# Token blocks of 384 in the second product, and a different order of the float64 pieces in the first step

## The chip, the cores and the metric

The kernel runs on one core of a Trainium2 chip. The metric is the device time of one execution in microseconds (us), the median of several runs. PE is the matrix engine (TensorE) and PEld its weight loads, which run beside its products. DVE (VectorE), ACT (ScalarE) and POOL (GpSimd) are the elementwise engines, SP issues the transfers (DMA). Matrix products are written to banks of PSUM, from which only DVE and ACT read here.

## The reference

```python
def sm_attn(qq, kk, vv):                      # scale = 1/8
    s = scale * np.matmul(qq, kk.transpose(0, 1, 3, 2))
    s = s - np.max(s, axis=-1, keepdims=True)
    a = np.exp(s)
    a = a / (np.sum(a, axis=-1, keepdims=True) + 1e-09)
    return np.matmul(a, vv)
...
p_packed = sm_attn(p, k, v)                   # q, k, v: 8 x 8 x 576 x 64, p: 8 x 8 x 32 x 64
out = sm_attn(q, p_packed, p_packed)
...
x = attn_out.transpose(0, 2, 1, 3).reshape(4608, 512)
x = (x @ w_a) * (x @ w_b) @ w_out             # 512 -> 1536 -> 512
h = x @ w_in                                  # 512 -> 2048
return (h * np.clip(h + 3.0, 0.0, 6.0) / 6.0) @ w_out2   # 2048 -> 512
```

The weights of the three dense products arrive as float64 and are rounded on the chip.

## The kernel before

The kernel has two halves. The first does the attention and the gated product with `w_a`, `w_b` and `w_out`; the second does `w_in`, the gate and the last product, with sums of blocks in place of some products. The change is in the first half.

**The first half.** The 4608 tokens are four groups `g` of two batch entries `b`, 576 tokens each. A step `t` is one group and one of the 12 slices of 128 of the middle width 1536, so there are 48 steps. The attention weights of a batch entry (`at`, on 256 rows, as a high and a low part `at_hi`, `at_lo`) are not multiplied with the packed values first. Instead `pw_unit` forms, for a step, the packed values times the weights `w_a` and `w_b` (`pw`, split into `pw_hi` and `pw_lo`), and `ab_unit` multiplies this with the attention weights. Each product of two split operands is three matrix products, high by high, high by low and low by high (`mm3`, lines 59 to 61).

A step has four `ab` units, two for each batch entry (`b` 0 or 1, half `h` 0 or 1). Before, each unit covers 288 tokens: two banks of six products, ACT copies the first bank to `a` (line 434), DVE multiplies `a` with the second bank to `g32` (line 436), and two ticks later ACT rounds to `g_hi` (line 442) and POOL forms `g_lo` (line 443). A tick is a counter that is advanced after every unit of PE work. There are three banks for `ab`, two for `y` (the second product) and three shared ones (`att`), of which a `pw` takes two.

**The second product.** `y_unit` takes three steps at a time: for one 128-slice `oc` of the 512 outputs and one token block `r` it makes nine products of 128 x 128 weights with the block of `g`. Before, a block is 288 tokens, four blocks for a group. The sum over the four sets of three steps stands in `acc` (lines 460 to 463) and goes to DRAM as `y1d`.

**Float64 pieces.** A piece is 128 x 512 of a weight matrix in float64. Rounding one takes two passes on ACT (lines 81, 82), three on DVE (lines 84, 88, 93) and one on POOL (line 96). Pieces `(m, 0)` and `(m, 1)` are the two halves of the `w_a` and `w_b` slice of step m, `(m, 2)` is its slice of `w_out`. All of them are rounded in the first 12 steps (group 0), a step ahead of use or more; five come even before step 0. `wo_split` then splits a `w_out` slice into a high and a low part.

**Order.** Every engine works through its own list in the order of the program; the loop over steps writes that order by hand. In each step come the units `ab` (0,0), `pw` of the next step, `ab` (0,1), `ab` (1,0), `ab` (1,1). After each there are two slots into which parts of pieces (`parts`), units of the next group's attention (`todo`) and a `y` unit are put. Some units of steps 0 and 1 are done ahead, in a prologue.

Of the kernel before, what the change touches and what calls it, by code (L numbers as in the profile page):

```python
# [8 lines left out]
F32 = mybir.dt.float32  # L9
F32R = mybir.dt.float32r  # L10
# [9 lines left out]
B, H, S, D, NP = 8, 8, 576, 64, 32  # L20
NT = B * S
DM, F1, F2 = 512, 1536, 2048
P = 128
NM1 = F1 // P
NM2 = F2 // P
SH = S // 2
NG = B // 2
TG = 2 * S
SW = 3
# [11 lines left out]
def f32(ap):  # L41
    return ap.bitcast(F32)
# [3 lines left out]
def tile_kernel(ctx: ExitStack, tc: tile.TileContext, qT, kT, vn, pT, wab, wo1, win, wo2, out):  # L46
# [9 lines left out]
    act, dve, pool, pe, sp = nc.scalar, nc.vector, nc.gpsimd, nc.tensor, nc.sync  # L56
# [223 lines left out]
    def at_split(b, cs=(0, 1)):  # L280
        if b not in at_t:
            at_t[b] = (
                main.tile([P, 2, S], F32R, tag="at_hi", name=f"at_hi{b}", bufs=3),
                main.tile([P, 2, S], F32R, tag="at_lo", name=f"at_lo{b}", bufs=3),
            )
        hi, lo = at_t[b]
        for c in cs:
            a = at32_t.pop((b, c))
            act.copy(hi[:, c, :], a)
            pool.tensor_sub(lo[:, c, :], a, f32(hi[:, c, :]))  # L290

    def loads(b):

# [33 lines left out]


    first = [(0, 0), (0, 1), (1, 0), (1, 1), (2, 0)]
    pieces = first + [(2, 1), (0, 2), (1, 2), (3, 0)]  # L330
    for m in range(1, NM1):
        pieces += [x for x in ((m + 2, 1), (m + 1, 2), (m + 3, 0)) if x[0] < NM1]
    n_first = len(pieces)
    pieces += [(NM1 + m, w) for m in range(NM2) for w in range(2)]
    raw64 = {}
# [85 lines left out]
    def ab_unit(t, b, h):  # L421
        hi, lo = pw_t[t]
        ath, atl = at_t[2 * (t // NM1) + b]
        r = 2 * b + h
        ps = []
        for w in range(2):
            pt = psum.tile([P, 512], F32, tag="ab", name=f"ab{t}_{r}{w}", bufs=BANKS["ab"])[:, :SH]
            for c in range(2):
                ws = slice(w * P, (w + 1) * P)
                ts = slice(h * SH, (h + 1) * SH)  # L430
                mm3(pt, hi[:, c, b, ws], lo[:, c, b, ws], ath[:, c, ts], atl[:, c, ts], c == 0, c == 1)
            ps.append(pt)
        a = main.tile([P, SH], F32, tag="a", name=f"a{t}_{r}", bufs=2)
        act.copy(a, ps[0])  # L434
        g32 = main.tile([P, SH], F32, tag="g32", name=f"g32_{t}_{r}", bufs=3)
        dve.tensor_mul(g32, a, ps[1])  # L436
        gh = main.tile([P, SH], F32R, tag=f"g_hi{r}", name=f"g_hi{t}_{r}", bufs=SW + 1)
        gl = main.tile([P, SH], F32R, tag=f"g_lo{r}", name=f"g_lo{t}_{r}", bufs=SW + 1)
        g_t[t, r] = (gh, gl)

        def rest():
            act.copy(gh, g32)  # L442
            pool.tensor_sub(gl, g32, f32(gh))  # L443
            if t % SW == SW - 1:
                later(2, lambda: y_ready.extend((t // NM1, t % NM1 // SW, oc, r) for oc in range(DM // P)))

        later(2, rest)

    y_ready = []

    def y_unit(g, s, oc, r):
        ps = psum.tile([P, 512], F32, tag="y", name=f"y{g}_{s}{oc}{r}", bufs=BANKS["y"])[:, :SH]
        for i in range(SW):
            t = g * NM1 + s * SW + i
            gh, gl = g_t[t, r]
            oh, ol = wo_t[t, oc // 2]
            ws = slice(oc % 2 * P, (oc % 2 + 1) * P)
            mm3(ps, oh[:, ws], ol[:, ws], gh, gl, i == 0, i == SW - 1)
        if s == 0:
            acc_t[oc, r] = main.tile([P, SH], F32, tag=f"acc{oc}{r}", name=f"acc{g}_{oc}{r}", bufs=1)  # L460
            act.copy(acc_t[oc, r], ps)
        else:
            dve.tensor_add(acc_t[oc, r], ps, acc_t[oc, r])  # L463
        if s == NM1 // SW - 1:
            sp.dma_start(y1d[oc, :, g * TG + r * SH:g * TG + (r + 1) * SH], acc_t[oc, r])

# [125 lines left out]
    def spread(work, n):  # L592

        return [work[len(work) * i // n:len(work) * (i + 1) // n] for i in range(n)]
# [69 lines left out]
    def ahead_by_one(starts):  # L664
# [8 lines left out]
            units.append(unit)  # L673
        return units

    for t in range(NSTEP):
        g, m = divmod(t, NM1)
        if m == 0 and g + 1 < NG:
            lhs_tiles(g + 1)
            b = 2 * g + 2  # L680
            u0, u1 = att_units(b), att_units(b + 1)
            bg = u0 + u1[:1] + [lambda b=b: at_split(b, (0,))] + u1[1:2] + [lambda b=b: at_split(b, (1,))] + u1[2:]
        if m == 0 and g + 1 == NG:
            sp.dma_start(*stores[-1])
            es_att.close()
            p2a = es_p2a.enter_context(tc.tile_pool(name="p2a", bufs=1, side="right", reuse_waits="tile"))
            y_load, y_first, y_part = y_units(p2a, 0)
            wo_load0, wo_parts0 = wo_prep(p2a, 0)
# [13 lines left out]

        if t == 0:
            n_conv = 4
        elif g == 0:
            n_conv = sum(x < NM1 for x in (m + 2, m + 1, m + 3))
        else:
            n_conv = 2 * NM2 * (t - NM1 + 1) // (2 * NM1) - 2 * NM2 * (t - NM1) // (2 * NM1) if g < 3 else 0
        parts = spread(list(range(5 * n_conv)), 9 if n_conv > 2 else 6) + [[]] * 4
        now = []  # L710
        for i, (u, *x) in enumerate(units):
            if (u.__name__[:2], *x) not in ahead:
                u(*x)
            tick()
            if i == 1:
                wab_load(t + 3)
            if m % SW < 2 and i in ((3, 4) if t == 0 else (1, 2)):
                wo_split(t, i - (3 if t == 0 else 1))
            if m % SW == 1 and i == 4:
                wo_split(t + 1, 0)  # L720
            if m % SW == 2 and i == 1:
                wo_split(t, 1)
            if i in (3, 4) and m == NM1 - 1 and g + 1 < NG:
                at_split(2 * g + 3, (i - 3,))
            for k in range(2):
                for _ in parts[2 * i + k]:
                    if not now:
                        now = piece_units()
                    now.pop(0)()
                for fn in todo[2 * i + k]:  # L730
                    fn()
                if y_ready and (k == 0 or i in (1, 3)):
                    y_unit(*y_ready.pop(0))
                    tick()
    while due or y_ready:
# [193 lines left out]
```

## Time and profile before

| | |
|---|---|
| median of 3 runs | 1561.6 us (1560.71 to 1562.37) |
| the profiled execution | 1560.16 us, of which the trace's span is 1558.4 us |
| PE busy | 1491.6 us, 96% of the span |
| DVE, ACT, POOL busy | 56%, 44%, 32% of the span |
| mean granted clock of PE | 0.986 of full speed |

A matrix product is pipelined, so the time that PE is called busy overlaps itself: what one product takes out of the engine's time is the distance from its start to the next start, not its duration. An engine's idle time costs something only where another engine, in the end PE, waits for it. Names are tiles of the program without their numbers; "y<-g_hi,wo_hi" is a product that writes a `y` bank. A row that ends in [7.66 <-ACT ex] says that the engine stood idle for 7.66 us before it and what ended that.

### The profile page before, as it was taken

To read this page: it belongs to the slowest core of one execution; us is meant where nothing else is said; L and a number is where in the kernel's file an instruction comes from. 1 tells how busy PE (TensorE), PEld (TensorE's weight loads), DVE (VectorE), ACT (ScalarE), POOL (GpSimd) and SP (SyncE) were. 2 spreads that over 40 slices of the span, in tenths; PEclk is the share of its full clock that TensorE was granted. 3 is DMA by queue.
4 is the path that set the end of the run, shared out by engine and by line. 5 is a ranking of instruction groups with operands and counts; after the bars stand their busy time and mean duration, and the time that the engine had idled before them with its cause. 6 is when DMAs were issued, how large, how long until landed. Compare 5 with 4: busy or idle time off the path is not lost. (4 is left out here: it accounts for less than half of the span.)

```text
span 1558.4 us, 27988 instructions
## 1 busy us (share of the span) xinstructions
PE 1491.6 (96%) x11128; PEld 1349.4 (87%) x11128; DVE 879.5 (56%) x1591; ACT 684.0 (44%) x1453; POOL 493.7 (32%) x484
## 2 busy tenths in 40 slices
PE   5498999999999999999999999999999999999998
PEld 2387999889989899999989988998998998998997
DVE  5788885565755566545545464465455446446443
ACT  4466644554545454454524343343343334334332
POOL 2567554454543545555622140030020011011000
PEclk9799999999999999999999999999999999999999
DMA  8674464644466432755353435243334243333331
GB/s 287 222 235 163 159 202 149 209 149 156 142 204 183 158 105 95 262 187 197 113 190 140 172 135 183 95 183 135 142 138 180 96 181 136 141 139 135 140 140 41
DMA packets 75954, 250.06 MB, mean 160 GB/s; under 512 B 7856, under 2 KB 26288, under 8 KB 68784
## 3 DMA queue, kind: packets, MB, share of 16 engines
q1 hardware_dynamic: 75824, 248.28, 45.8%
q8 instruction: 87, 1.43, 0.4%
q14 instruction: 43, 0.35, 0.1%
HBM read 196.87 MB, written 51.38 MB: 159 GB/s over the span
## 5 line engine op out<-in xcount | busy, mean ns | idle before, releaser
L59 PE MATMUL ab<-at_hi,pw_hi 128*128 128x288 f32 x768 | 234.5, 305 | 8.6 <-ACT a L434 5.3
L59 PE MATMUL y<-g_hi,wo_hi 128*128 128x288 f32 x768 | 232.1, 302 | 1.8 <-DVE acc L463 1.6
L61 PE MATMUL ab<-at_hi,pw_lo 128*128 128x288 f32 x768 | 229.3, 299 | 4.3 <-DVE pw_lo L414 4.3
L60 PE MATMUL ab<-at_lo,pw_hi 128*128 128x288 f32 x768 | 228.9, 298 | 1.8 <-POOL at_lo L290 1.8
L60 PE MATMUL y<-g_lo,wo_hi 128*128 128x288 f32 x768 | 227.7, 296 | 0.4 <-POOL g_lo L443 0.4
L61 PE MATMUL y<-g_hi,wo_lo 128*128 128x288 f32 x768 | 226.7, 295 | 0.0
L60 PE MATMUL o<-wo_lo,g2h 128*128 128x512 f32 x576 | 225.0, 391 | 0.0
L61 PE MATMUL o<-wo_hi,g2l 128*128 128x512 f32 x576 | 224.9, 390 | 0.0
L59 PE MATMUL o<-wo_hi,g2h 128*128 128x512 f32 x576 | 224.7, 390 | 0.0
L443 POOL TENSOR_TENSOR g_lo<-g,g_hi 128x288 fp32r<-128x288 f32 x192 | 164.4, 859 | 172.9 <-ACT g_hi L442 171.1
L777 DVE TENSOR_TENSOR g2l<-u,g2h 128x384 fp32r<-128x384 f32 x192 | 121.9, 635 | 141.0 <-ACT g2h L776 136.0
L436 DVE TENSOR_TENSOR g<-a,ab 128x288 f32<-128x288 f32 x192 | 86.3, 450 | 170.7 <-PE ab L61 116.1
L59 PEld LDWEIGHTS ab<-at_hi,pw_hi 128*128 128x128 f32 x768 | 146.6, 191 | 24.7 <-ACT a L434 7.7
L59 PEld LDWEIGHTS y<-g_hi,wo_hi 128*128 128x128 f32 x768 | 145.0, 189 | 19.2 <-DVE acc L463 8.6
L768 ACT ACTIVATE r<-c,half_b 128x384 f32<-128x384 f32 x144 | 89.2, 620 | 144.7 <-DVE c L761 144.2
L61 PEld LDWEIGHTS ab<-at_hi,pw_lo 128*128 128x128 f32 x768 | 146.7, 191 | 4.6 <-DVE pw_lo L414 4.5
L60 PEld LDWEIGHTS ab<-at_lo,pw_hi 128*128 128x128 f32 x768 | 146.8, 191 | 2.3 <-POOL at_lo L290 2.3
L569 POOL TENSOR_TENSOR ty_T<-raw_y 128x768 f32<-128x768 f32 x12 | 23.4, 1953 | 386.6 <-DMA raw_y<-y1d 386.6
L60 PEld LDWEIGHTS y<-g_lo,wo_hi 128*128 128x128 f32 x768 | 145.2, 189 | 0.6 <-POOL g_lo L443 0.6
L434 ACT COPY a<-ab 128x288 f32<-128x288 f32 x192 | 76.3, 401 | 158.1 <-PE ab L61 156.7
L61 PEld LDWEIGHTS y<-g_hi,wo_lo 128*128 128x128 f32 x768 | 145.1, 189 | 0.0
L776 ACT CAST g2h<-u 128x384 fp32r<-128x384 f32 x192 | 99.2, 517 | 85.5 <-DVE u L770 84.1
(322 smaller groups left out, 3064.8 us busy)
## 6 DMA issues: line engine op xcount, KB each, us to landing
w<-w2d SPq DMA_DIRECT2D x47, 1792.0 KB, 7.2
rab<-wabf SPq DMA_DIRECT2D x36, 512.0 KB, 5.4
f64p<-in_wo SPq DMA_DIRECT2D x28, 512.0 KB, 3.7
w2d<-w SPq DMA_DIRECT2D x8, 1792.0 KB, 6.7
f64p<-in_wab SPq DMA_DIRECT2D x24, 512.0 KB, 3.9
k<-in_kT SPq DMA_DIRECT2D x16, 576.0 KB, 5.3
q<-in_qT SPq DMA_DIRECT2D x16, 576.0 KB, 5.2
ro<-wo1f SPq DMA_DIRECT2D x36, 256.0 KB, 3.3
```

What stands on the lines that cost most here:

```text
L59: pe.matmul(ps, lhsT=l_hi, rhs=r_hi, start=first, stop=False, skip_group_check=skip)
L60: pe.matmul(ps, lhsT=l_hi, rhs=r_lo, start=False, stop=False, skip_group_check=skip)
L61: pe.matmul(ps, lhsT=l_lo, rhs=r_hi, start=False, stop=last, skip_group_check=skip)
L434: act.copy(a, ps[0])
L436: dve.tensor_mul(g32, a, ps[1])
L443: pool.tensor_sub(gl, g32, f32(gh))
L569: pool.tensor_sub(z[to], get(a), get(b))
L768: act.activation(r, c, AF.Relu, bias=half_b, scale=1.0 / 6.0)
L776: act.copy(hi, u)
L777: dve.tensor_sub(lo, u, f32(hi))
```

## The change

It has two parts. First, a token block of the second product is 384 tokens (`TY`), three blocks for a group. The `ab` units follow: unit (0,0) covers tokens 0 to 384 of the first batch entry, (0,1) the other 192, (1,0) the first 192 of the second entry and (1,1) its last 384; the two units of 192 fill one block of `g` together. ACT now copies straight into `g32` (four buffers in place of three, `a` is gone) and DVE multiplies in place.

Second, step 0 rounds two pieces in place of four, and the `w_out` slices are rounded in the step that uses them, or one step later for the first, in place of a step ahead. The total is the same: steps 9 and 11 round one more. A `y` unit is put only into the first of the two slots of a unit, and only if its `w_out` part is there. In the prologue one low part of the second batch entry's attention weights is made on DVE in place of POOL.

```diff
@@ constants @@
+TY = 384
+
+UNIT = {
+    (0, 0): (0, TY, 0, 0), (0, 1): (TY, S, 1, 0),
+    (1, 0): (0, S - TY, 1, S - TY), (1, 1): (S - TY, S, 2, 0),
+}
@@ at_split @@
-            pool.tensor_sub(lo[:, c, :], a, f32(hi[:, c, :]))
+
+            (dve if b == 1 and c == 0 else pool).tensor_sub(lo[:, c, :], a, f32(hi[:, c, :]))
@@ order of the pieces @@
-    pieces = first + [(2, 1), (0, 2), (1, 2), (3, 0)]
-    for m in range(1, NM1):
-        pieces += [x for x in ((m + 2, 1), (m + 1, 2), (m + 3, 0)) if x[0] < NM1]
+    by_step = [[(2, 1), (3, 0)], [(0, 2), (3, 1), (1, 2)]]
+    by_step += [[(m, 2)] + [(m + 2, i) for i in range(2) if m + 2 < NM1] for m in range(2, NM1)]
+    pieces = sum(by_step, first)
@@ ab_unit @@
-        r = 2 * b + h
+        t0, t1, r, r0 = UNIT[b, h]
+        n = t1 - t0
...
-                mm3(pt, hi[:, c, b, ws], lo[:, c, b, ws], ath[:, c, ts], atl[:, c, ts], c == 0, c == 1)
+                mm3(pt, hi[:, c, b, ws], lo[:, c, b, ws], ath[:, c, t0:t1], atl[:, c, t0:t1], c == 0, c == 1)
...
-        a = main.tile([P, SH], F32, tag="a", name=f"a{t}_{r}", bufs=2)
-        act.copy(a, ps[0])
-        g32 = main.tile([P, SH], F32, tag="g32", name=f"g32_{t}_{r}", bufs=3)
-        dve.tensor_mul(g32, a, ps[1])
+        g32 = main.tile([P, TY], F32, tag="g32", name=f"g32_{t}_{b}{h}", bufs=4)[:, :n]
+        act.copy(g32, ps[0])
+        dve.tensor_mul(g32, g32, ps[1])
@@ y_unit @@
-        ps = psum.tile([P, 512], F32, tag="y", name=f"y{g}_{s}{oc}{r}", bufs=BANKS["y"])[:, :SH]
+        ps = psum.tile([P, 512], F32, tag="y", name=f"y{g}_{s}{oc}{r}", bufs=BANKS["y"])[:, :TY]
@@ the loop over steps @@
-        if t == 0:
-            n_conv = 4
-        elif g == 0:
-            n_conv = sum(x < NM1 for x in (m + 2, m + 1, m + 3))
+        if g == 0:
+            n_conv = len(by_step[m])
...
-                if y_ready and (k == 0 or i in (1, 3)):
+                if y_ready and k == 0 and (y_ready[0][0] * NM1 + y_ready[0][1] * SW + SW - 1, y_ready[0][2] // 2) in wo_t:
```

The instruction lists show what this moves. On PE, in step 0, this stood at the border of units (1,0) and (1,1); `ab_21` is the second bank of the one, `ab_30` the first of the other:

```order
L59 MATMUL ab_21_646<-at_hi_631,pw_hi_453 128x288
L60 MATMUL ab_21_646<-at_lo_632,pw_hi_453 128x288
L61 MATMUL ab_21_646<-at_hi_631,pw_lo_454 128x288
L59 MATMUL ab_30_661<-at_hi_631,pw_hi_453 128x288
L60 MATMUL ab_30_661<-at_lo_632,pw_hi_453 128x288
L61 MATMUL ab_30_661<-at_hi_631,pw_lo_454 128x288
```

At the same border of the changed kernel stands this (`ab_101` and `ab_110`, lines 66 to 68 are 59 to 61 of before):

```order
L66 MATMUL ab_101_642<-at_hi_627,pw_hi_453 128x192
L67 MATMUL ab_101_642<-at_lo_628,pw_hi_453 128x192
L68 MATMUL ab_101_642<-at_hi_627,pw_lo_454 128x192
L66 MATMUL ab_110_654<-at_hi_627,pw_hi_453 128x384
L67 MATMUL ab_110_654<-at_lo_628,pw_hi_453 128x384
L68 MATMUL ab_110_654<-at_hi_627,pw_lo_454 128x384
```

The number of products, and of weight loads, is the same; half of them are 192 tokens wide and half 384.

On DVE, behind the last multiplication of step 0, this stood before (`cv_a` are the passes of pieces, `mx` and `nb` belong to the first softmax of batch entry 2; two pieces more stand ahead of these rows):

```order
L84 TENSOR_SCALAR cv_ap_2_745<-f64p_2_709 128x512
L88 SCALAR_TENSOR_TENSOR cv_ap_2_745<-f64p_2_709,cv_ap_2_745 128x512
L93 SCALAR_TENSOR_TENSOR cv_ap_2_745<-cv_sqp_2_742,cv_ap_2_745 128x512
L84 TENSOR_SCALAR cv_ap_0_775<-f64p_0_711 128x512
L88 SCALAR_TENSOR_TENSOR cv_ap_0_775<-f64p_0_711,cv_ap_0_775 128x512
L93 SCALAR_TENSOR_TENSOR cv_ap_0_775<-cv_sqp_0_772,cv_ap_0_775 128x512
L193 TENSOR_REDUCE mx_787<-ex_733 128x1
L195 TENSOR_SCALAR nb_789<-mx_787 128x1
```

In the changed kernel the same place reads as follows, from the last multiplication on:

```order
L443 TENSOR_TENSOR g_0_11_668<-g_0_11_668,ab_111_661 128x384
L91 TENSOR_SCALAR cv_ap_1_693<-f64p_1_451 128x512
L95 SCALAR_TENSOR_TENSOR cv_ap_1_693<-f64p_1_451,cv_ap_1_693 128x512
L100 SCALAR_TENSOR_TENSOR cv_ap_1_693<-cv_sqp_1_690,cv_ap_1_693 128x512
L91 TENSOR_SCALAR cv_ap_0_711<-f64p_0_587 128x512
L95 SCALAR_TENSOR_TENSOR cv_ap_0_711<-f64p_0_587,cv_ap_0_711 128x512
L100 SCALAR_TENSOR_TENSOR cv_ap_0_711<-cv_sqp_0_708,cv_ap_0_711 128x512
L200 TENSOR_REDUCE mx_747<-ex_723 128x1
L202 TENSOR_SCALAR nb_749<-mx_747 128x1
```

Two pieces stand ahead of `mx`, not four.

On ACT, in step 14 (the second group), this stood behind the rounding of a `pw` (the two rows with `pw_hi`); `a_1` and `a_2` are the copies of units (0,1) and (1,0):

```order
L410 CAST pw_hi_3873<-pw_1_3876 128x512
L442 CAST g_hi_0_3858<-g_14_0_3856 128x288
L391 CAST wo_hi_3899<-ro_3555 128x256
L81 ACTIVATE cv_sqp_1_3908<-f64p_1_3053 128x512
L82 ACTIVATE p2f_1_3907<-f64p_1_3053 128x512
L434 COPY a_1_3929<-ab_10_3915 128x288
L434 COPY a_2_3959<-ab_20_3945 128x288
```

In the changed kernel:

```order
L418 CAST pw_hi_3604<-pw_1_3607 128x512
L452 CAST g_hi_0_3591<-g_14_00_3588 128x384
L399 CAST wo_hi_3630<-ro_3305 128x256
L88 ACTIVATE cv_sqp_1_3639<-f64p_1_2973 128x512
L89 ACTIVATE p2f_1_3638<-f64p_1_2973 128x512
L442 COPY g_14_01_3660<-ab_010_3646 128x192
L442 COPY g_14_10_3689<-ab_100_3675 128x192
```

The order is the same and the widths differ.

## Rows read from the trace of the kernel before

**Rows 1.** The page: engines' busy time, and granted clock in 40 equal slices.
```profile
PE 1491.6 (96%) x11128; PEld 1349.4 (87%) x11128; DVE 879.5 (56%) x1591; ACT 684.0 (44%) x1453; POOL 493.7 (32%) x484
PEclk9799999999999999999999999999999999999999
```

**Rows 2.** The page's groups of instructions: count, busy us, mean ns, idle before.
```profile
L59 PE MATMUL ab<-at_hi,pw_hi 128*128 128x288 f32 x768 | 234.5, 305 | 8.6 <-ACT a L434 5.3
L59 PE MATMUL y<-g_hi,wo_hi 128*128 128x288 f32 x768 | 232.1, 302 | 1.8 <-DVE acc L463 1.6
```

**Rows 3.** Timeline of PE in step 37: start us, duration us, instruction.
```profile
643.95 0.30 PE L59 MATMUL y<-g_hi,wo_hi 128*128 128x288 f32 x1
...
646.34 0.29 PE L59 MATMUL ab<-at_hi,pw_hi 128*128 128x288 f32 x1
```

**Rows 4.** Timeline of PE in the second half, blocks of 384 and 512.
```profile
899.69 0.33 PE L59 MATMUL h_6z<-yh_B,w 128*128 128x384 f32 x1
...
900.73 0.39 PE L59 MATMUL o<-wo_hi,g2h 128*128 128x512 f32 x1
...
904.82 0.34 PE L59 MATMUL h_7x<-yh_B,w 128*128 128x384 f32 x1
```

**Rows 5.** Timeline at 650.6 us, behind an idle time: weight loads, then PE.
```profile
650.63 0.19 PEld L59 LDWEIGHTS ab<-at_hi,pw_hi 128*128 128x128 f32 x1 [0.41 <-DVE g L436]
650.74 0.19 PEld L60 LDWEIGHTS ab<-at_lo,pw_hi 128*128 128x128 f32 x1
...
650.63 0.40 PE L59 MATMUL ab<-at_hi,pw_hi 128*128 128x288 f32 x1
650.87 0.29 PE L60 MATMUL ab<-at_lo,pw_hi 128*128 128x288 f32 x1
```

**Rows 6.** The transposes `et` of 128 columns: the tile's view (min/median/max ns), and PE's timeline.
```profile
L204 PEld LDWEIGHTS et<-ident,ex x48: 137/140/231, 11.9 to 558.6; 128*128 128x128 f32 x48
L204 PE MATMUL et<-ident,ex x48: 270/272/477, 11.9 to 558.7; 128*128 128x128 f32 x48
...
170.98 0.49 PE L204 MATMUL et<-ident,ex 128*128 128x128 f32 x3
```

**Rows 7.** Engines in a stretch of step 0: busy us (instructions), clock, DMA share, GB/s.
```profile
69.40:77.00 7.60, 0.00 (x0) 0.00 (x0) 7.29 (x10) 3.89 (x9) 5.36 (x5) 0.50 0.90 303
```

**Rows 8.** Timelines of DVE, ACT and PE in step 0.
```profile
63.20 0.68 DVE L84 TENSOR_SCALAR cv_ap<-f64p 128x512 uint32<-128x512 uint32 x1
...
68.70 0.42 DVE L84 TENSOR_SCALAR cv_ap<-f64p 128x512 uint32<-128x512 uint32 x1
...
75.11 0.74 DVE L193 TENSOR_REDUCE mx<-ex 128x1 f32<-128x576 f32 x1
...
76.13 0.78 ACT L199 ACTIVATE ex<-ex,nb 128x576 f32<-128x576 f32 x1 [2.83 <-DVE nb L195]
...
77.06 0.90 PE L204 MATMUL et<-ident,ex 128*128 128x128 f32 x3 [7.66 <-ACT ex L199]
```

**Rows 9.** PE's waits from 0 to 60 us: us in total, times, longest.
```profile
PE ab L60 <- POOL at_lo L290: 1.8, 2, 1.1
```

**Rows 10.** PE's waits from 85 to 800 us.
```profile
PE s L176 <- DVE pw_lo L414: 8.1, 4, 4.1
PE ab L59 <- ACT a L434: 5.3, 9, 0.7
PE y L59 <- DVE acc L463: 1.6, 2, 1.3
```

**Rows 11.** Timelines of PE and ACT behind a `pw` in step 35, and of ACT in step 38.
```profile
607.78 0.40 PE L59 MATMUL ab<-at_hi,pw_hi 128*128 128x288 f32 x1
...
611.14 0.40 PE L59 MATMUL ab<-at_hi,pw_hi 128*128 128x288 f32 x1 [0.71 <-ACT a L434]
...
610.70 0.69 ACT L434 COPY a<-ab 128x288 f32<-128x288 f32 x2
...
652.40 0.41 ACT L434 COPY a<-ab 128x288 f32<-128x288 f32 x1
```

More of the change, by code (lines that the diff above doesn't have):

```diff
@@ L423, in ab_unit @@
         ath, atl = at_t[2 * (t // NM1) + b]
-        r = 2 * b + h
+        t0, t1, r, r0 = UNIT[b, h]
+        n = t1 - t0
         ps = []
         for w in range(2):
-            pt = psum.tile([P, 512], F32, tag="ab", name=f"ab{t}_{r}{w}", bufs=BANKS["ab"])[:, :SH]
+            pt = psum.tile([P, 512], F32, tag="ab", name=f"ab{t}_{b}{h}{w}", bufs=BANKS["ab"])[:, :n]
             for c in range(2):
                 ws = slice(w * P, (w + 1) * P)
-                ts = slice(h * SH, (h + 1) * SH)
-                mm3(pt, hi[:, c, b, ws], lo[:, c, b, ws], ath[:, c, ts], atl[:, c, ts], c == 0, c == 1)
+                mm3(pt, hi[:, c, b, ws], lo[:, c, b, ws], ath[:, c, t0:t1], atl[:, c, t0:t1], c == 0, c == 1)
             ps.append(pt)
-        a = main.tile([P, SH], F32, tag="a", name=f"a{t}_{r}", bufs=2)
-        act.copy(a, ps[0])
-        g32 = main.tile([P, SH], F32, tag="g32", name=f"g32_{t}_{r}", bufs=3)
-        dve.tensor_mul(g32, a, ps[1])
-        gh = main.tile([P, SH], F32R, tag=f"g_hi{r}", name=f"g_hi{t}_{r}", bufs=SW + 1)
-        gl = main.tile([P, SH], F32R, tag=f"g_lo{r}", name=f"g_lo{t}_{r}", bufs=SW + 1)
-        g_t[t, r] = (gh, gl)
+        g32 = main.tile([P, TY], F32, tag="g32", name=f"g32_{t}_{b}{h}", bufs=4)[:, :n]
+        act.copy(g32, ps[0])
+        dve.tensor_mul(g32, g32, ps[1])
+        if r0 == 0:
+            g_t[t, r] = (
+                main.tile([P, TY], F32R, tag=f"g_hi{r}", name=f"g_hi{t}_{r}", bufs=SW + 1),
+                main.tile([P, TY], F32R, tag=f"g_lo{r}", name=f"g_lo{t}_{r}", bufs=SW + 1),
+            )
+        gh, gl = (x[:, r0:r0 + n] for x in g_t[t, r])
         def rest():
@@ L443, in rest @@
             pool.tensor_sub(gl, g32, f32(gh))
-            if t % SW == SW - 1:
+            if t % SW == SW - 1 and r0 + n == TY:
                 later(2, lambda: y_ready.extend((t // NM1, t % NM1 // SW, oc, r) for oc in range(DM // P)))
@@ L459, in y_unit @@
         if s == 0:
-            acc_t[oc, r] = main.tile([P, SH], F32, tag=f"acc{oc}{r}", name=f"acc{g}_{oc}{r}", bufs=1)
+            acc_t[oc, r] = main.tile([P, TY], F32, tag=f"acc{oc}{r}", name=f"acc{g}_{oc}{r}", bufs=1)
             act.copy(acc_t[oc, r], ps)
@@ L464, in y_unit @@
         if s == NM1 // SW - 1:
-            sp.dma_start(y1d[oc, :, g * TG + r * SH:g * TG + (r + 1) * SH], acc_t[oc, r])
+            sp.dma_start(y1d[oc, :, g * TG + r * TY:g * TG + (r + 1) * TY], acc_t[oc, r])
     PROD = {1: (0, "B11"), 2: (1, "B21"), 3: (6, "B22"), 4: (2, "T4"), 5: (3, "T1"), 6: (4, "T2"), 7: (5, "T3")}
@@ L674, in ahead_by_one @@
         return units
+    splits = {(1, 3): [(0, 0)], (1, 4): [(0, 1)], (2, 0): [(1, 0)], (2, 1): [(1, 1)]}
+    splits |= {(t, 2 + c + (t % SW < 2)): [(t, c)] for t in range(2, NM1) for c in range(2)}
     for t in range(NSTEP):
@@ L701, in tile_kernel @@
         ]
-        if t == 0:
-            n_conv = 4
-        elif g == 0:
-            n_conv = sum(x < NM1 for x in (m + 2, m + 1, m + 3))
+        if g == 0:
+            n_conv = len(by_step[m])
         else:
             n_conv = 2 * NM2 * (t - NM1 + 1) // (2 * NM1) - 2 * NM2 * (t - NM1) // (2 * NM1) if g < 3 else 0
-        parts = spread(list(range(5 * n_conv)), 9 if n_conv > 2 else 6) + [[]] * 4
+        parts = spread(list(range(5 * n_conv)), 9 if n_conv > 2 else 6 if g > 0 or n_conv == 2 else 3) + [[]] * 7
         now = []
@@ L716, in tile_kernel @@
                 wab_load(t + 3)
-            if m % SW < 2 and i in ((3, 4) if t == 0 else (1, 2)):
-                wo_split(t, i - (3 if t == 0 else 1))
-            if m % SW == 1 and i == 4:
+            if g == 0:
+                for x in splits.get((t, i), ()):
+                    wo_split(*x)
+            elif m % SW < 2 and i in (1, 2):
+                wo_split(t, i - 1)
+            elif m % SW == 1 and i == 4:
                 wo_split(t + 1, 0)
-            if m % SW == 2 and i == 1:
+            elif m % SW == 2 and i == 1:
                 wo_split(t, 1)
```

## The prediction, made before the changed kernel had run

> **What bounds the kernel now.** I read the page first. PE is busy 96% of the span and its clock stands at 0.9 or more in all but one of 40 slices, while no other engine reaches 60% [rows 1]. So the kernel is PE's own stream of products, plus what PE loses by waiting in the first 140 us. An edit counts if it shortens PE's stream or a wait of PE; work taken off DVE, ACT or POOL elsewhere is worth nothing.
>
> PE's stream is read from starts, not from durations. Two `y` units, 18 products of 288 tokens, take 643.95 to 646.34, or 0.1328 us from start to start [rows 3]. Six products of 384 take 0.1733 us each and eighteen of 512 take 0.2272 us [rows 4]. The three lie on a line: 0.421 ns for a column and about 12 ns for each product whatever its width. A wider product spreads the 12 ns over more columns; that is all the second product can win.
>
> The waits come next. In step 0 PE does nothing from 69.4 to 77.0 us while DVE is busy for 7.29 of these 7.60 us [rows 7]. The chain is in the timelines: DVE starts a first piece at 63.20, a third at 68.70, and only behind the fourth, at 75.11, the maximum `mx`; ACT's exponential waits for that until 76.13 and PE's transpose until 77.06 [rows 8]. From 85 to 800 us PE's waits are small, 8.1 us for `pw_lo`, 5.3 for ACT's copies and 1.6 for `acc` [rows 10].
>
> **The second product.** There are 768 products on each of three lines [rows 2], 2304 in all, and 1728 of them are left at 384. 2304 x 0.1328 = 306.0 us, 1728 x 0.1733 = 299.5: **-6.5 us**. The banks and `acc` tiles become wider and fewer; what DVE and ACT do there lies beside PE's products.
>
> **The `ab` products.** Their number stays at 2304. Half go to 384 tokens: 1152 x 0.1733 = 199.6 us. The other half go to 192, and no product of this kind with 192 columns is in the trace. The line would give 0.1733 - 192 x 0.000421 = 0.0925 us, 106.6 us together, and the sum of 306.2 would be that of before (306.0). But every product brings its own weight load of 128 x 128, and a load takes time too. Behind an idle time, with nothing to hold it up, the second load starts 0.11 us after the first, and the first product's record is 0.40 us long where the next has 0.29, since it waits 0.11 us for its weights [rows 5]. In the stream the next load starts with the current product and is ready 0.11 us later, unseen under 0.133. Under 0.0925 it would be seen. The transposes, which pair a load of 128 columns with only 128 moving columns, go at (0.49 - 0.272) / 2 = 0.109 us [rows 6]. These two rows are nearest, so I take 0.108 us: 1152 x 0.108 = 124.4, sum 324.0, **+18.0 us**. The lower bound is the line (+0.2). The upper is that 192 columns cost as much as 288 do now, 0.1328: 153.0 us, +46.6; above it nothing points, since 288 columns already go at that rate with the same loads.
>
> The load record of these operands is 0.19 us long [rows 5], against 140 ns for the transposes' [rows 6], which speaks rather for more than 0.108 than for less. The Trainium skill, "TensorE: Matmul & The Clock Gate", section "LDWEIGHTS (loading the stationary operand)", gives a load as its number of columns over 1.2, that is 107 ns for 128 columns; the spacing of 0.11 us agrees. By that figure the term would be an estimated +16.9 us in place of +18.0.
>
> **New waits in PE's stream.** In one step of three, units (0,1) and (1,0) follow each other and the `pw` directly. The second bank of (1,0) reuses the bank that ACT's copy of (0,1) must empty, and ACT has `pw_hi`, `g_hi`, `wo_hi` and often a piece ahead of it. In step 35 the two copies run from 610.70, and PE waits 0.71 us for the first [rows 11]. PE reaches that point after 18 products, so at 0.108 in place of 0.1328 it is there 18 x 0.0248 = 0.45 us earlier, and ACT's list ahead is as long as before. The 5.3 us are nine waits of at most 0.7 [rows 10], so about seven full ones: 7 x 0.45 = 3.1. In steps without a piece the copy runs from 652.40 for 0.41 us [rows 11], 2.18 us behind the first product's start at 650.63 [rows 5]; PE would be there at 0.107 + 1.94 = 2.05, and waits some 0.2 us in five such steps. Together **+4 us**; bounds 0 (ACT's shorter copies and the `wo_hi` that moves behind them in the first group make up for it) and 8 (each wait doubles). Queued behind the stalled product are only PE's own, no other engine.
>
> **The first step.** A piece in this crowded stretch costs DVE (68.70 - 63.20) / 2 = 2.75 us for the first two, and (75.11 - 68.70) / 2 = 3.2 for the next two [rows 8]. With two left, `mx` follows at about 68.8, where the third piece began. Its inputs, ACT's copies of the scores, lose the piece between them, so they are there. The exponential, which came 1.0 us behind `mx`, is free at 69.8, ahead of ACT's `pw_hi`, and the transpose at 70.7 in place of 77.06: **-6.4 us**. What is late next is the second exponential, behind a piece on ACT and DVE as before, and it moves with the first. Bounds: 0, if DVE's list of the next steps (three pieces each, as before) takes the time back, and -9 if the clock, at 0.50 (its level of 1.2 GHz) in this stretch [rows 7], also rises earlier; since PE idles before 69 us in any case, I count nothing for the clock. The two pieces go to steps 9 and 11, where DVE, with a total of 56% [rows 1], hides their 5.5 us; uncovered they would cost those.
>
> The low part on DVE in the prologue cuts PE's two waits for `at_lo`, 1.8 us [rows 9]: POOL's two passes were in series. I take **-0.8**, between 0 and -1.8.
>
> **Small terms.** Where PE waits for DVE's `pw_lo` (8.1 us, four times), slower `ab` products before it are hidden: -1, bounds 0 and -1.4 (four steps of 24 x 0.0155 = 0.37). `y` units no longer follow each other, so the 1.6 us for `acc` mostly go: -1, bounds 0 and -1.6 [rows 10]. The `y` units wait for their `wo` part in the program's order only, and 12 in 15 slots of three steps fit. `g32` has one buffer more and `a` none; the copy now waits for POOL's `g_lo` of four units earlier, which is behind PE by two ticks: nothing. The DMA transfers of `y1d` are fewer and larger, hidden. The second half is untouched.
>
> **Sum.** -6.5 + 18.0 + 4 - 6.4 - 0.8 - 2 = +6.3 us. The profiled execution took 1560.2 us with what lies around its span, 1.4 below the median of 1561.6. So 1566.5 against it, and **1568 us** for a median.
>
> **Rivals.** (A) *Faster: the load hides.* The spacing of 0.11 us was seen only from standstill; if loads in a stream run further ahead, 192 columns go at 0.0925. Against it: no load in the stream starts before the product ahead of it. Then the term is +0.2; PE reaches ACT's bank 18 x 0.040 = 0.73 us earlier, so the waits grow by 5 in seven steps and 2.5 in five, and the sum is -6.5 + 0.2 + 7.5 - 7.2 - 1 = -7.0: 1554.6 us. It decides in favour of the change once a 192 product is under about 0.102. The Trainium skill, the same page, section "Back-to-back issue gap", says that spacing is set by load and product together but puts 128 columns at about 81 ns, which is this rival's side; no row here shows such a rate for these operands.
>
> (B) *Much slower: 192 columns cost as much as 288.* For it, the load record of 0.19 us; against it, the spacing of 0.11. -6.5 + 46.6 + 0 - 7.2 - 2 = +30.9: 1592 us.
>
> (C) *Step 0 gains nothing*, since DVE's list is full until the 90s and the 6.4 us come back as a wait for `pw_lo`: +12.7, 1574 us. DVE's idle time of the later steps speaks against it.
>
> (D) *About the same*: the clock rises earlier with PE's work in step 0 (-9), and ACT's waits do not grow (0): -6.5 + 18.0 - 9 - 0.8 - 2 = -0.3, 1561 us.
>
> **Chances.** My forecast 0.36, its own range 1564 to 1574; A 0.33; D 0.16; C 0.08; B 0.07. A run of this kernel varies by about 0.1%, so 0.2% (3.1 us) is about what can be told from no change. Faster is A, 0.33; same is D and the lower edge of the forecast, 0.18; slower is the rest, 0.49. The range goes to 1551, below A by half of its waits' growth, and to 1588, which leaves out B and the upper end of the unknown gap.
>
> **What would show it.** The starts of the 192 products in the changed kernel's timeline: 0.108 for the forecast, 0.093 for A, 0.13 for B. The six products of 384 beside them at 0.173. The transpose of step 0 near 71 us. PE's wait for ACT's copy (`ab` behind line 442), 5.3 us now, near 9. The end of the first half, near 800 us now, some 6 us later. I am wrong if the 192 products keep to the line, or if a wait outside these places appears, for instance ACT waiting for POOL over a `g32` buffer.

## The result, and the profile after

The changed kernel takes 1578.8 us (median of four runs, 1575.5 to 1583.6), the kernel before 1562.0 beside it. The ratio is 1.011, with a 95% interval of 1.0089 to 1.0131: **16.8 us slower**, where 6.3 were forecast. The profiled execution took 1578.6 us; the rows below are read from it. Its executions differ by up to 8 us among themselves, so a time read from one trace is good to a few us.

The starts of all products in the trace, from one to the next and summed by what the first of the two writes, give the first half (up to the first `h_0x`, the first product of the second half) as follows. The last column holds the terms of the prediction's sum that fall there; the waits for `at_lo` and most of those for `acc` stand between `ab` products or behind one.

| us | before | after | difference | forecast |
|---|---|---|---|---|
| `ab`, with the waits behind it | 335.5 | 357.0 | +21.5 | +18.0 +4 -0.8 -1 |
| `y` | 317.9 | 315.6 | -2.3 | -6.5 |
| everything else | 147.8 | 138.1 | -9.7 | -6.4 -1 |
| end of the first half | 801.2 | 810.7 | +9.5 | +6.3 |
| second half, to the last product's start | 752.1 | 760.5 | +8.4 | 0 |

So the first half came out 3.2 us above the sum, and about half of the loss is in code that the change does not touch. The page and two of its groups, which answer to [rows 1, 2]:

```profile
PE 1511.4 (96%) x10552; PEld 1363.8 (86%) x10552; DVE 857.6 (54%) x1544; ACT 679.8 (43%) x1437; POOL 488.1 (31%) x483
...
PEclk9899999999999999999999999999999999999999
...
L66 PE MATMUL ab<-at_hi,pw_hi 128*128 128x192 f32 (+1 forms) x768 | 239.6, 312 | 11.7 <-ACT g L442 8.6
...
L66 PE MATMUL y<-g_hi,wo_hi 128*128 128x384 f32 x576 | 199.9, 347 | 0.5 <-ACT wo_hi L399 0.5
```

The products themselves, against [rows 3, 5]. PE's timeline in step 27, a bank of 192 columns and behind it a `y` unit:

```profile
491.50 0.27 PE L66 MATMUL ab<-at_hi,pw_hi 128*128 128x192 f32 x1
491.61 0.28 PE L67 MATMUL ab<-at_lo,pw_hi 128*128 128x192 f32 x1
491.72 0.27 PE L68 MATMUL ab<-at_hi,pw_lo 128*128 128x192 f32 x1
491.83 0.36 PE L66 MATMUL y<-g_hi,wo_hi 128*128 128x384 f32 x1
492.03 0.34 PE L67 MATMUL y<-g_lo,wo_hi 128*128 128x384 f32 x1
492.21 0.34 PE L68 MATMUL y<-g_hi,wo_lo 128*128 128x384 f32 x1
```

192 columns start every 0.11 us (median 0.111 over the kernel), 384 every 0.173 in a stream; the first step of the `y` unit is 0.20. In step 0, against [rows 8]:

```profile
65.80 0.41 DVE L91 TENSOR_SCALAR cv_ap<-f64p 128x512 uint32<-128x512 uint32 x1
...
68.61 0.74 DVE L200 TENSOR_REDUCE mx<-ex 128x1 f32<-128x576 f32 x1
...
69.63 0.78 ACT L206 ACTIVATE ex<-ex,nb 128x576 f32<-128x576 f32 x1
...
70.56 0.90 PE L211 MATMUL et<-ident,ex 128*128 128x128 f32 x3 [0.31 <-ACT ex L206]
```

The maximum follows the second piece, and the transpose starts at 70.56 in place of 77.06. PE's waits from 85 to 800 us, against [rows 10]:

```profile
PE ab L66 <- ACT g L442: 8.6, 8, 2.1
PE s L183 <- DVE pw_lo L422: 6.7, 4, 2.8
PE pw L416 <- POOL rab L103: 0.8, 1, 0.8
PE y L68 <- POOL wo_lo L400: 0.6, 2, 0.4
PE y L66 <- ACT wo_hi L399: 0.5, 1, 0.5
```

The last three, waits for pieces that are rounded late, are not in the kernel before.

In the second half one wait of PE has grown. In the kernel before it reads

```profile
PE h_1x L59 <- ACT s L839: 1.7, 6, 0.6
```

and in the changed kernel

```profile
PE h_1x L66 <- ACT s L854: 7.0, 6, 2.4
```

ACT's copy `s` empties a bank at the start of a tile of 768 tokens (there are six tiles, counted here from 0). It stands behind ACT's copies `os` of the last tile's output, and those wait for one of three buffers, that is, for an output transfer to land. The start of tile 3 in the changed kernel:

```profile
1198.30 0.57 ACT L808 COPY os<-o 128x512 f32<-128x512 f32 x1
...
1199.62 5.93 SPq L811 DMA_DIRECT2D out<-os  x6
...
1203.34 0.58 ACT L808 COPY os<-o 128x512 f32<-128x512 f32 x1 [4.47 <-DMA out<-os]
...
1205.00 0.48 ACT L854 COPY s<-h_1x 128x384 f32<-128x384 f32 x1
1205.54 0.44 PE L66 MATMUL h_1x<-yh_B,w 128*128 128x384 f32 x1 [1.61 <-ACT s L854]
```

The row to look at is the second of ACT, with 4.47 us of idle time before it: its buffer is late, the copy `s` behind it is late, and PE stands. In the kernel before ACT waits 2.92 us at this place.

Behind the wait of 2.4 us at the start of tile 4 PE's granted clock also falls to 0.50 (its level of 1.2 GHz) for 3.4 us; behind that at the start of tile 2 it does the same, behind that of tile 3 it stays at 1.00. The stretch at tile 4, first in the changed kernel, then in the kernel before (columns as in [rows 7]):

```profile
1329.00:1336.00 7.00, 4.57 (x17) 3.95 (x16) 2.27 (x4) 2.60 (x6) 0.00 (x0) 0.76 0.69 229
```

```profile
1314.00:1321.00 7.00, 6.80 (x36) 6.05 (x35) 3.65 (x7) 2.62 (x6) 0.00 (x0) 1.00 0.94 331
```

Tiles 2, 3 and 4 take 127.7, 125.9 and 128.1 us, where those of the kernel before take 124.4 or 124.5.

### The profile page after: what moved, and what is told of

It is laid out like the page before. It is cut to its first block, busy times and chain, and to the rows that moved or that the text cites. A ratio compares the mean times of both kernels' runs of the same rounds, so it can differ in the third digit from the quotient of the medians.

```text
span 1576.8 us, 26746 instructions
## 1 busy us (share of the span) xinstructions
PE 1511.4 (96%) x10552; PEld 1363.8 (86%) x10552; DVE 857.6 (54%) x1544; ACT 679.8 (43%) x1437; POOL 488.1 (31%) x483
## 4 chain that ended last, share of the span: by engine, by line
PE 86%; DVE 4%; ACT 3%; DMA 3%; POOL 2%; issue 2%; SPq 0%; ACTq 0%; DVEq 0%; POOLq 0%
PE o L67 8%; PE o L68 8%; PE o L66 7%; PE y L66 7%; PE ab L66 7%; PE y L68 6%; PE ab L68 6%; PE y L67 6%; PE ab L67 6%; PE pw L416 3%; DMA out<-os 1%; PE s L183 1%; PE pv L233 1%; DMA k<-in_kT 1%; ACT r L783 0%
## 5 line engine op out<-in xcount | busy, mean ns | idle before, releaser
L66 PE MATMUL ab<-at_hi,pw_hi 128*128 128x192 f32 (+1 forms) x768 | 239.6, 312 | 11.7 <-ACT g L442 8.6
L68 PE MATMUL ab<-at_hi,pw_lo 128*128 128x192 f32 (+1 forms) x768 | 236.2, 308 | 4.7 <-DVE pw_lo L422 4.6
L67 PE MATMUL ab<-at_lo,pw_hi 128*128 128x192 f32 (+1 forms) x768 | 236.0, 307 | 1.2 <-POOL at_lo L298 0.7
L453 POOL TENSOR_TENSOR g_lo<-g,g_hi 128x384 fp32r<-128x384 f32 (+1 forms) x192 | 161.3, 842 | 221.0 <-ACT g_hi L452 213.1
L66 PE MATMUL y<-g_hi,wo_hi 128*128 128x384 f32 x576 | 199.9, 347 | 0.5 <-ACT wo_hi L399 0.5
L68 PE MATMUL y<-g_hi,wo_lo 128*128 128x384 f32 x576 | 194.6, 338 | 0.6 <-POOL wo_lo L400 0.6
L67 PE MATMUL y<-g_lo,wo_hi 128*128 128x384 f32 x576 | 193.9, 337 | 0.0
L443 DVE TENSOR_TENSOR g<-g,ab 128x384 f32<-128x384 f32 (+1 forms) x192 | 86.0, 448 | 178.5 <-PE ab L68 105.6
L452 ACT CAST g_hi<-g 128x384 fp32r<-128x384 f32 (+1 forms) x192 | 83.7, 436 | 115.9 <-DVE g L443 115.4
L68 PEld LDWEIGHTS o<-wo_hi,g2l 128*128 128x128 f32 x576 | 108.6, 188 | 23.3
```

Source lines behind the costliest of these rows:

```text
L66: pe.matmul(ps, lhsT=l_hi, rhs=r_hi, start=first, stop=False, skip_group_check=skip)
L67: pe.matmul(ps, lhsT=l_hi, rhs=r_lo, start=False, stop=False, skip_group_check=skip)
L68: pe.matmul(ps, lhsT=l_lo, rhs=r_hi, start=False, stop=last, skip_group_check=skip)
L443: dve.tensor_mul(g32, g32, ps[1])
```

## The experiments

Each was timed in five rounds against the kernel before on the same chip. "First half" and "second half" are read from the trace as in the table above.

| run | time | ratio, 95% interval | first half | second half |
|---|---|---|---|---|
| pieces only | 1556.6 | 0.9967 (0.9954 to 0.9979) | 797.7 | 752.4 |
| blocks only | 1585.5 | 1.0157 (1.0142 to 1.0172) | 820.6 | 759.7 |
| `ab` 288, `y` 384 | 1577.9 | 1.0112 (1.0099 to 1.0125) | 811.4 | 759.1 |
| cuts at 320 and 224 | 1585.8 | 1.0172 (1.0155 to 1.0189) | 817.4 | 759.9 |
| half weights | 1570.6 | 1.0051 (1.0037 to 1.0065) | 804.6 | 757.9 |
| changed kernel + 64 products | 1579.8 | 1.0109 (1.0092 to 1.0126) | 815.4 | 760.4 |
| changed kernel + 128 | 1581.6 | 1.0129 (1.0111 to 1.0146) | 816.0 | 757.3 |
| kernel before + 64 | 1561.3 | 0.9998 (0.9989 to 1.0008) | 802.7 | 751.8 |
| changed kernel + 32 | 1574.8 | 1.0093 (1.0077 to 1.0108) | 814.8 | 752.4 |
| kernel before + 32 | 1567.0 | 1.0042 (1.0028 to 1.0056) | 804.3 | 758.6 |
| ring for `g` | 1577.7 | 1.0110 (1.0095 to 1.0125) | 811.6 | 760.1 |
| ring, tile `a`, + 32 | 1569.6 | 1.0054 (1.0038 to 1.0069) | 808.0 | 752.5 |

**One part alone: the pieces.** The `ab` and `y` units of before, with the order of pieces, the splits and the low part on DVE of the changed kernel.

```diff
-TY = 384
-UNIT = {...}
+(ab_unit and y_unit of before, blocks of 288)
-if y_ready and k == 0 and (...) in wo_t:
+if y_ready and (k == 0 or i in (1, 3)) and (...) in wo_t:
```

> The second part of the change alone: all blocks stay at 288 tokens, step 0 rounds two pieces, the w_out slices later, one low part on DVE. Theory (the terms of the sum are independent): the transpose of step 0 comes 6 to 7.5 us earlier and most of it is kept, so -5 to -8 us against before, about 1555 us; the end of the first half near 795 us, the second half as long as before (757 us). Rival 1 (the pieces come back later as waits for pw_lo): -2 to +1 us. Rival 2 (the second half is slower whenever its start is shifted): the second half grows by some 8 us here too, and the sum is 0 to +3.

Faster by 0.33%, 5 us by the ratio, which is the near edge of the theory, and by 3.6 us at the end of the first half, which lies between the theory and its first rival. The transpose starts at 73.09 us, not at 70.56, since here PE waits 2.3 us for the low part that DVE makes (at 60.29 us) and runs at a granted clock of 0.72 behind it (60 to 66 us; 1.00 in the kernel before). The second half is as before, so a shifted start does not lengthen it.

**The other part alone: the blocks.** The kernel before with `TY`, `UNIT` and the new `ab_unit` and `y_unit`.

```diff
+TY = 384
+UNIT = {...}
+(ab_unit and y_unit of the changed kernel)
-if y_ready and (k == 0 or i in (1, 3)):
+if y_ready and k == 0:
```

> The first part of the change alone: blocks of 384 and ab units of 384 and 192, with the pieces in the order of before. Theory (192-wide products start every 0.111 us because their weight load takes that long; blocks alone decide the loss): the first half grows by 15 to 20 us, PE still idles before the transpose of step 0 at 77 us, and a time of 1577 to 1582 us if the second half is as before. Rival 1 (the longer second half belongs to the blocks): 8 us more, 1585 to 1590. Rival 2 (the two parts interact, and much of the loss comes from w_out slices that are rounded late): +8 to +12 only, 1570 to 1574.

The first half grows by 19.3 us, as the theory has it, and the second by 7.6, as its first rival has it: both hold. The blocks make the whole loss; the pieces win in either kernel, 3.6 us with the old blocks and 9.9 with the new (820.6 to 810.7), by one trace each.

**The blocks of 384 without the products of 192.** The cut between two `ab` units is a number, and `g` is rounded in pieces into the blocks of 384 that a unit covers (one `y` slot more).

```diff
-        t0, t1, r, r0 = UNIT[b, h]
+        t0, t1 = (0, CUT[b]) if h == 0 else (CUT[b], S)    # CUT = (288, 288)
...
-            act.copy(gh, g32)
-            pool.tensor_sub(gl, g32, f32(gh))
+            for gh, gl, s, r, full in parts:
+                act.copy(gh, s)
+                pool.tensor_sub(gl, s, f32(gh))
```

> The changed kernel with ab units of 288 again, whose g is written in pieces into the blocks of 384 (ACT and POOL round two pieces for the two middle units). Theory (the loss is the 192-wide products): ab products start every 0.133 us as before, y products keep 0.174, so -2 to -6 for y and -5 to -8 for step 0 against before: 1548 to 1555 us, the best of the kernels. Rival 1 (the loss is in the y products or the order of slots): 1565 to 1575 us. Rival 2 (ACT's two more copies in a step make PE wait): as the theory, with PE waits for ACT's copies of 15 us and more, 1560 us.

The theory fails as a forecast of the time, and the rivals' times are too short as well; the second half is 7.0 us longer than before. `ab` products do start every 0.133 us again, and `y` takes 310.8 us, but the first half is no shorter than that of the changed kernel: PE waits 11.7 us for ACT's copies and 4.3 for DVE's `t`, and ACT itself waits 61 us (15 times) to write `g_hi` until the `y` units have read the old one.

**Other widths.** The same with `CUT = (320, 224)`.

> As the kernel with 288 again, but the ab units of the first batch entry are 320 and 256 tokens and those of the second 224 and 352. Theory (a weight load of 0.111 us is a floor under the line of 0.421 ns a column and 12 ns): start to start 0.147, 0.120, 0.111 and 0.160 us, so ab costs 3 to 4 us more than with 288, and the time is 3 to 5 us above that kernel. Rival 1 (narrow products have a cost of their own that grows below 288): 256 at 0.125 or more and 224 at 0.118 or more, 8 us and more above. Rival 2 (no floor, the 0.111 of 192 came from waits): 0.106 for 224, and the same time as with 288.

Start to start (medians): 320 columns 0.147 us, 256 columns 0.120, 224 columns 0.112, 352 columns 0.167. 256 and 320 lie on the line; 224 does not (the line gives 0.106), so a floor begins between 224 and 256, at about 0.11. The 352 are 0.007 above the line, which nothing here explains, and the time is 7.9 us above that of the kernel with 288 where 3 to 5 were expected; 6.0 of them are in the first half.

**The load by itself.** In the 192-wide units the second of three products gets 64 columns of weights; half the rows of that product are left out.

```diff
+                half = P // 2 if n < TY else P
-        pe.matmul(ps, lhsT=l_hi, rhs=r_lo, ...)
+        pe.matmul(ps[:half], lhsT=l_hi[:, :half], rhs=r_lo, ...)
```

> The changed kernel, in which the second of each three products (high by low) of the 192-wide ab units has only 64 columns of weights in place of 128; it leaves out half of that product's rows. Theory (a product of 192 columns waits for its weight load, 0.111 us for 128 columns): from the first to the second product of the three 0.093 us, the line's value, in place of 0.111, the other two starts as before, and 384 x 0.018 = 7 us less, 1572 us. Rival 1 (192 columns take 0.111 us by themselves): all three starts stay at 0.111 and the time at 1579. Rival 2 (a load takes the same for 64 columns): the same.

PE's timeline with its loads:

```profile
491.59 0.19 PEld L66 LDWEIGHTS ab<-at_hi,pw_hi 128*128 128x128 f32 x1
491.68 0.27 PE L66 MATMUL ab<-at_hi,pw_hi 128*128 128x192 f32 x1
491.70 0.14 PEld L67 LDWEIGHTS ab<-at_lo,pw_hi 128*64 128x64 f32 x1
491.79 0.25 PE L67 MATMUL ab<-at_lo,pw_hi 128*64 128x192 f32 x1
491.79 0.19 PEld L68 LDWEIGHTS ab<-at_hi,pw_lo 128*128 128x128 f32 x1
491.88 0.27 PE L68 MATMUL ab<-at_hi,pw_lo 128*128 128x192 f32 x1
```

Behind a load of 128 columns the next load starts 0.11 us later, behind the one of 64 after 0.09, and each product starts 0.09 behind its own load. So the short step is from the second to the third product (median 0.087), not from the first to the second as expected, but it is there, and the first half is 6.1 us shorter, of 7 expected. So it is not the 192 columns that set the pace of 0.111 us, but the weights. That it is their load, as the loads' starts suggest, and not the product's number of rows is argued: the run halves both.

**Where the second half's time goes.** In the traces so far the longer second halves had a fetch of 16 KB of instructions (queue `q8 instruction` in the DMA view) among the output transfers at the start of two or three tiles, the short ones not. The number of fetches goes with PE's instructions: 87 for 22,256 products and loads in the kernel before, 83 for 21,104 in the changed one, 254 to 256 each. The blocks of 384 take 1152 products and loads out of the first half, four and a half fetches, so every later fetch should fall half a distance from where it fell. (The count is not all: the run with half weights, with as many instructions as the changed kernel, has the fetches at tiles 1 and 2 in place of 2 to 4, and a second half of 757.9 us. Why is open.) To move it, small products were added where PE waits in the prologue (N = 64, 128 and 32).

```diff
             ps = bank(f"bd{b}")
+            for j in range(N if b == 1 else 0):
+                q = j % 4
+                pe.matmul(ps[NP * q:NP * q + NP, :64], lhsT=z["et"][0][:, 0, NP * q:NP * q + NP],
+                          rhs=v_t[b, 0][:, 0, 64 * q:64 * q + 64], start=True, stop=True)
```

> The changed kernel with 64 small products more (128 instructions of PE with their loads) in the prologue, where PE waits from 31.9 to 35.1 us. In the four kernels with blocks of 384 a fetch of 16 KB of instructions falls into the output transfers at the borders of the tiles 1 to 3 of the second half, in the two with 288 it does not; 1152 fewer instructions are four and a half fetches of 256. Theory (the position of the instruction fetch makes the second half longer): the fetches move by half a distance, the second half takes 752 to 753 us in place of 760.5, PE waits about 2 us for the copies s in place of 7, and the time is 1570 to 1572 us. Rival (the blocks of 384 make the second half longer in another way, by what they leave in DRAM or in SBUF): 759 to 761 us and 1578 to 1580.

> The same with 128 small products, 256 instructions, which is one whole fetch: the fetches fall where they fell in the changed kernel. Theory (position of the fetch): second half 759 to 761 us as in the changed kernel, time 1578 to 1581. If it is short here too, what helped in the run with 64 was something else than the position.

> The kernel before with 64 small products more in the same place, nothing else. Theory (position of the fetch): the fetches move by half a distance into the output transfers, and the second half takes 759 to 760 us in place of 752.1, the time is 1567 to 1570 us. Rival (the second half depends on the blocks): 752 us and 1561.

With 64 the second half stayed long in the changed kernel (760.4 us; 757.3 with 128) and short in the kernel before (751.8), against the theory as it was put. The count was wrong: each of these float32 products is two products with two loads in the trace, so 64 were 256 instructions, a whole fetch, and the fetches fell among the transfers of the same tiles as before, or of none. For the second half the three runs are controls: added work by itself does not make it short or long. With 128 it is 3 us shorter, about 2 of them because the granted clock does not fall behind a wait. The first half is no clean control: in the changed kernel it ends 4.1 to 5.3 us later with products added, in the kernel before 1.5 (64) and 3.1 (32). The granted clock then falls at other places of the first 80 us; why is not shown. Then half as many:

> The changed kernel with 32 small products more. The trace of the run with 64 counts each of these float32 products as two records with two loads, so 64 were 256 instructions, one whole fetch, and 128 two; 32 are 128 instructions, half a fetch. Theory (position of the fetch): now the fetches move away from the output transfers, second half 752 to 753 us in place of 760.5, PE waits about 2 us for the copies s, time 1570 to 1573 us. Rival (the blocks of 384 make the second half longer in another way): 759 to 761 us and 1578 to 1581.

> The kernel before with 32 small products more, nothing else: half a fetch. Theory (position of the fetch): the fetches move into the output transfers at three or four borders, the second half takes 757 to 761 us in place of 752.1, the time is 1566 to 1570 us. Rival: 752 us and 1561.

Both came out as the theory has it: the changed kernel's second half fell to 752.4 us, and the kernel before, with nothing else changed, rose to 758.6. The total of the former is 2 us above its range, since its first half ended 4.1 us later than that of the changed kernel; its ratio (1.0077 to 1.0108) is not clear of the changed kernel's (1.0089 to 1.0131), so the gain is shown by the second half alone. The loss of the kernel before with 32 is clear in the time too. The wait of PE, first in the changed kernel with 32, then in the kernel before with 32:

```profile
PE h_1x L66 <- ACT s L858: 2.2, 6, 0.8
```

```profile
PE h_1x L59 <- ACT s L843: 7.3, 6, 2.1
```

The DMA view of six us from the first output transfer on, at the start of tile 3; the GB/s row is the stretch in 40 slices. The changed kernel:

```profile
GB/s 0 0 0 0 0 96 382 451 328 382 383 355 355 369 369 383 396 355 341 178 27 27 27 14 27 27 27 27 27 0 0 0 0 0 137 382 396 410 314 192
...
q8 instruction: 1, 0.02, 1.1%
...
out<-os SPq DMA_DIRECT2D x6, 256.0 KB, 3.1
```

The changed kernel with 32 products more:

```profile
GB/s 0 0 0 0 0 0 314 410 382 355 383 383 410 355 382 383 423 341 382 314 28 0 0 0 96 382 396 341 396 137 232 369 355 410 396 342 382 410 328 205
...
out<-os SPq DMA_DIRECT2D x6, 256.0 KB, 2.2
```

With the fetch, the first three transfers end in a tail of 27 GB/s for nine slices of 0.15 us, about a fourteenth of the rate ahead of it: it looks as if one of the 16 engines still had its share to move. Over all 14 traces, the tiles 1 to 4 are 56 lengths from tile start to tile start; the 26 with such a fetch 1.0 to 2.7 us behind the first output transfer take 125.8 to 128.1 us, the 30 without 124.4 to 125.2. The 26 fall into two groups: 19 in which the granted clock stays at 1.00 take 125.8 to 126.5, and 7 in which it falls to 0.50 for 3.4 us behind PE's wait take 127.7 to 128.1.

**What holds the kernels with 288 and 384 back.** First, `g` in one ring of four steps, so that each unit is rounded in one piece and `y` units may take the slots of before.

```diff
+            g_t["hi"] = main.tile([P, SW + 1, TG], F32R, tag="g_hi", name="g_hi", bufs=1)
...
+        gh, gl = (g_t[k][:, t % (SW + 1), x0:x1] for k in ("hi", "lo"))
```

> ab units of 288 and y blocks of 384 once more, but g stands in one ring of four steps with 1152 tokens each, so that ACT and POOL round each unit in one piece, as many copies as before, and y units may take the slots that they took before. Theory (the loss of the changed kernel's first half is the 192-wide products, and that of the first kernel with 288 was its added copies): the first half is 7 to 11 us shorter than before, 790 to 794 us, PE's waits for ACT's copies 4 to 8 us; the second half 757 to 760, since PE has as many instructions as the changed kernel; 1554 to 1560 us. Rival (blocks of 384 make ACT late in any case): waits for ACT's copies over 10 us, first half over 803, time over 1566.

Then also the tile `a` of before, and the 32 products:

```diff
-        act.copy(g32, ps[0])
-        dve.tensor_mul(g32, g32, ps[1])
+        act.copy(a, ps[0])
+        dve.tensor_mul(g32, a, ps[1])
```

> The kernel with the ring, in which ACT copies the first bank to a tile of its own again (a, two buffers) and DVE multiplies into g32 (three buffers), as in the kernel before, so that ACT's copy does not wait for POOL; and with the 32 small products that move the fetches of instructions. Theory (copying straight into g32 ties ACT's copy, and so PE's bank, to POOL; that was the loss of the two kernels with ab units of 288 and y blocks of 384): first half 790 to 796 us, PE's waits for ACT's copies and for DVE's g under 8 us from 85 to 800 us, second half 752 to 753, time 1545 to 1552 us, the shortest of all. Rival (blocks of 384 with the y units in these slots make ACT and DVE late in the first group, whatever the buffers): first half 806 to 813, second half 752 to 753, time 1560 to 1568.

The rivals hold for the first half: 811.6 and 808.0 us, though `y` took 309.4 and 309.9, 8 us less than before. Not all their terms do: PE's waits for ACT's copies with the ring are 9.3 us, not over 10, and the time of the last kernel is 1.6 us above its rival's range. ACT's wait of 61 us for the old `g_hi` is gone with the ring and the first half is as long, so that was not the cause either. PE's waits from 85 to 800 us in the last kernel:

```profile
PE ab L63 <- ACT a L443: 9.4, 10, 2.6
PE s L180 <- DVE pw_lo L423: 6.9, 4, 2.7
PE s L180 <- DVE t L262: 6.5, 3, 3.9
PE ab L63 <- DVE g L445: 3.5, 3, 2.0
```

They are nearly the same without the tile `a` (9.3, 6.4, 6.4 and 3.4 us), so the copy straight into `g32` is not what is late. What is, stays open; the wait for `t` does not occur in the kernel before. The second half is 752.5 us, which the 32 products explain once more.

Of all kernels only the one with the pieces alone beats the kernel before.

## Why the prediction was right or wrong

**Direction right, size off by 10 us, half of the loss in another place.** The loss is 16.8 us against 6.3. The time of 1578.8 us is in the upper part of the full range (1551 to 1588), but above the forecast's own 1564 to 1574 and at no rival's time. That part of the range stood for `ab` products slower than 0.108 us, and most of the excess comes from elsewhere; that the time falls into it is luck. In the profiled executions 8.4 us more than forecast lie in the second half and 3.2 in the first, 4.2 of it in `y` alone; the 1 us by which this exceeds the difference of the medians is within the spread of the runs.

**The `ab` products: right.** 192 columns take 0.111 us against 0.108, which makes the term 3.5 us larger. That the weights set this pace, and not the columns, is shown by the nearly equal 0.111 and 0.112 us for 192 and 224 columns and by the run with half weights, whose first half is 6.1 us shorter. The Trainium skill, "TensorE: Matmul & The Clock Gate", "LDWEIGHTS (loading the stationary operand)", gives a load as its columns over 1.2, an estimated 107 ns for 128; the trace agrees within 4%. Rivals A (0.093) and B (0.13) fall. The Trainium skill, the same page, "Back-to-back issue gap", gives 81 ns for 128 columns, on rival A's side; no product of this kind with 128 columns was run, and those with 192 and 224 do not come near it.

**New waits of PE: the sum right, in part by luck.** PE waits 8.6 us for ACT's copies, of which about 9 had been forecast. Five of the waits grew much as worked out, from 0.7 to 1.08 us. But of the five new ones of 0.2 us only one shows (0.28), and 2.1 us of the sum stand in step 2, where the first group's pieces crowd ACT, and had not been forecast. The upper bound does not follow from its reason: 5.3 us of waits doubled are 5.3 us more, not 8.

**The second product: a term mis-sized.** "-6.5 us" took 0.1733 for every product. It holds within a stream, but the units no longer follow each other or units of the same width: 73 units behind 192-wide `ab` products take 1.60 us (median), 73 behind 384-wide ones 1.57, and nine products in a stream 1.56. The 73 units alone are 73 x 0.04 = 2.9 of the 4.2 us that are missing. Where the `ab` units have no 192 (the four kernels with 288 or with cuts at 320 and 224) `y` takes 309.4 to 310.8 us, 7 to 8 less than before. Measured here: -2.3.

**Step 0: right.** The maximum at 68.6 (68.8 forecast), the transpose at 70.56 (70.7). What followed moved with it: the `pw` of step 3 comes 7.5 us earlier and that of step 4 still 4.6, behind the wait of 2.1 us. Rival C falls. D's mechanism was there in part: the granted clock from 69.4 to 77 us is 0.80 in place of 0.50 [rows 7].

**The low part on DVE: right here, not alone.** PE's waits for `at_lo` up to 60 us, 1.8 before [rows 9], are

```profile
PE ab L67 <- POOL at_lo L298: 0.7, 1, 0.7
PE ab L67 <- DVE at_lo L298: 0.5, 1, 0.5
```

With blocks of 288 the same edit made PE wait 2.3 us, and in the changed kernel with 64 products more 2.2, so the blocks are not what decides.

**Small terms: about right, with new waits beside them.** PE waits 6.7 us for `pw_lo` in place of 8.1, and no more for `acc`; but 1.9 us of waits for pieces rounded late had been put at nothing. ACT waiting for POOL over a `g32` buffer, named as a sign of being wrong, occurs twice (2.0 us), and PE does not wait behind it.

**"The second half is untouched": the step that failed.** Its code is; its time is not. 1152 instructions fewer moved PE's instruction fetches among the output transfers, these landed up to 4.7 us after their issue (2.9 before), and ACT, the copy `s` and PE waited in turn, twice with a lower granted clock behind the wait. Both directions are shown by the runs with 32 products. About half of the loss has thus nothing to do with the blocks as such: with the fetches moved away the changed kernel's second half is as short as before.

## What to carry to other kernels

Here a product costs the longer of what its columns take and the distance at which weight loads start: before splitting work into unequal widths, look up how far apart loads start, and don't extend a line from wider products below that. Steady rates give an upper bound of what wider units save, since each unit that stands between units of another kind pays for its entry. When untouched code changes its time by a near-constant step for each repetition, compare where instruction fetches fall among latency-bound transfers, and move them by half a fetch and by a whole one as a control.

## What the runs showed of the hardware

A fetch of 16 KB of instructions among three or six output transfers of 256 KB costs 1.3 to 2.0 us of the tile here, because the transfers land late and a chain of three engines hangs on it, and 3.2 to 3.6 us where PE's granted clock falls behind the wait. The Trainium skill, "Runtime: NRT & Kernel Launch", "Instruction fetch mechanics", gives blocks of 16 KiB with 256 instructions, which the count of fetches bears out (254 to 256 each), and calls the cost of one mostly hidden; in this kernel it is hidden except where it meets transfers that an engine waits for.

A float32 product of 64 columns stands in the trace as two products with two loads, which the count of instructions has to allow for.
